# Attention decode gradient on one core: one head in 128 partitions, or two heads in 64 each

## The chip, the cores and the metric

The kernel runs on one core of a Trainium2 chip. The time is the device time in microseconds (us) of one execution. A profiled execution also gives a span, from the first instruction to the last, and a trace of every engine: TensorE (PE; its weight loads are listed as PEld), VectorE (DVE), ScalarE (ACT), GpSimd (POOL), and SyncE (SP), which here does nothing but issue DMA transfers. The transfers run on 16 DMA engines.

## The reference

Attention with a single query per head, and its gradient: 32 heads, 8192 keys, head dimension 128, all in bf16. Of the forward pass the output is returned, of the backward pass dQ, dK and dV.

```python
B, H, Sq, Skv, Dh = 1, 32, 1, 8192, 128

def _fwd_reference(q, k, v):
    scale = q.shape[-1] ** -0.5
    scores = jnp.einsum('bhqd,bhkd->bhqk', q, k) * scale
    attn = _softmax(scores, axis=-1)
    return jnp.einsum('bhqk,bhkd->bhqd', attn, v)
```

For one head, with p the softmax of scale times K q, and g the gradient that comes in: out = p V; dV = p g (an outer product of 8192 by 128); dp = V g; ds = scale times p times (dp minus the sum of p dp); dQ = ds K; dK = ds q (again an outer product). So K and V are read once (2 MB per head each), and dK and dV, just as large, are written: 268.4 MB in all.

## The kernel before, in words

One head at a time. A tile of K or V has 128 partitions of 64 rows (NT) of 128 numbers: partition p holds the rows 64p to 64p + 63 of the head, which lie together in memory, so a transfer is 128 rows of 16 KB. K has three such buffers, V two, and the results G_dk and G_dv have two each.

The program is written in the order in which the engines take it (a manual schedule): each engine works through its own instructions in the order of the text and waits at each for what it needs. A round of the loop over h (line 304) works on head h and finishes the head before it (p_ = h - 1):

- Scores of head h. DVE transposes K in four chunks of 16 rows (`k_blocks`, line 162, into one tile XK with a slice for each chunk), and TensorE multiplies each chunk with q, four matmuls per chunk (`k_scores`, line 177). A window of zeros around the q columns (`q_win`) steers each chunk to its own rows of one accumulator. Between the chunks, DVE takes dp of the head before back from PSUM (`v_back`, line 214), and TensorE sums p dp (`pd_sum`).
- ds of the head before (`ds_of`), its contraction with K for dQ (`dq_of`, line 231), and its outer product with q, in four quarters on DVE (`outer`, line 256), woven between the steps of the softmax of head h: maximum (lines 339 to 350), exponential on ACT (line 355), sum by a matmul with ones (line 356), reciprocal (line 369), p repeated four times along the row for DVE (line 371), and the window for the contraction (line 372).
- V of head h: TensorE transposes it as 32-bit words, 32 blocks of 128 by 128 (`v_transposes`, line 197), ACT copies them from PSUM to the tile XV (`v_copy`, line 188), TensorE contracts p with V (`contract`, line 231) and XV with g (`v_scores`, line 207). Meanwhile DVE makes dV in four quarters (`outer`, line 256) into G_dv.

The accumulators of the output and of dQ stay in PSUM for eight heads (ST), in other rows for each; after every eighth head they are copied and gathered by eight matmuls (`gather_copy`, `gather`, lines 238 to 247).

All large transfers are issued by SP, in the order of the text, and SP waits at each until its tile is free or ready. At the start: K of head 0 in four parts, V 0, K 1, V 1, and soon K 2. Then in each round: store dK of the head before (`outer`, line 266, after the last quarter; halves for the first and the last head), load K of h + 2 (line 81), store dV of h, load V of h + 2 (line 85, before the last quarter of dV). All go through one queue to the 16 DMA engines. A load has to wait until the buffer's last reader is done, a product until the store of the buffer's last content has landed.

Of the kernel before, what the change touches and what calls it, by code (L numbers as in the profile page):

```python
# [14 lines left out]

CH = 16
TB = 4
ST = 8
R = 4
# [6 lines left out]
def kernel(  # L26
# [14 lines left out]
    assert D == P and S % (P * CH) == 0 and H <= P  # L41
    NT = S // P
    NCH = NT // CH
    NQ = P // QD
    assert NCH == 4 and NQ == 4
    W = D // 2
    NB = W // QD
    scale = float(D) ** -0.5
# [4 lines left out]
    ktpool = ctx.enter_context(tc.tile_pool(name="ktp", bufs=1))  # L53
    gpool = ctx.enter_context(tc.tile_pool(name="gen", bufs=2))
    small = ctx.enter_context(tc.tile_pool(name="small", bufs=2))
    xvpool = ctx.enter_context(tc.tile_pool(name="xvp", bufs=1))
    single = ctx.enter_context(tc.tile_pool(name="single", bufs=1))
# [7 lines left out]
    NG = NT // 4  # L65
    NX = NT // 2
    Kt, Vt, XK, XV, st, acc, qd = {}, {}, {}, {}, {}, {}, {}

    def rows_of(x, h, c, parts):
        L = NT // parts  # L70
        return x[0, h].rearrange("(p n) d -> p n d", p=P)[:, c * L:(c + 1) * L, :]
# [5 lines left out]
    def load_k(h):  # L77
        Kt[h] = kpool.tile([P, NT, D], BF16, tag="K", name="Kt")
        parts = NCH if h == 0 else 1
        for c in range(parts):  # L80
            nc.sync.dma_start(slots(Kt[h], c, parts), rows_of(k, h, c, parts))

    def load_v(h):
        Vt[h] = vpool.tile([P, NT, D], BF16, tag="V", name="Vt")
        nc.sync.dma_start(Vt[h][:], rows_of(v, h, 0, 1))
# [7 lines left out]
    load_v(1)  # L93

# [7 lines left out]
    nc.vector.memset(ones_f[:], 1.0)  # L102
    do_win = consts.tile([P, H, 2, QD + 2], BF16)
    nc.gpsimd.memset(do_win[:], 0.0)
    wins = {}
    for which in ("p", "ds"):
        wins[which] = []
        for i in range(2):
            w = consts.tile([P, NG, 2 * QD - 4], BF16, name=f"win_{which}{i}")
            nc.gpsimd.memset(w[:], 0.0)  # L110
            wins[which].append(w)
    q_win = []
    for i in range(2):
        w = consts.tile([P, 2 * NB, P + QD], BF16, name=f"win_q{i}")
        nc.gpsimd.memset(w[:], 0.0)
        q_win.append(w)
# [3 lines left out]

    q_blk = consts.tile([P, H, 2 * NB, NQ], BF16)
    four = consts.tile([H, 2 * NB, NQ, QD], BF16)
# [12 lines left out]
    for c in range(2 * NB):  # L135
        nc.vector.tensor_tensor(
            q_blk[:, :, c, :], tp[:, c, 0:H].unsqueeze(2).to_broadcast([P, H, NQ]),
            in_quad[:].unsqueeze(1).to_broadcast([P, H, NQ]), op=ALU.mult)


    twice = consts.tile([H, 2, 2, W], BF16)

    def do_columns():
        for e2 in range(2):
            nc.scalar.copy(
                twice[:, e2], rows[:, 1, :].rearrange("h (j e) -> h e j", e=2)[:, e2:e2 + 1, :].to_broadcast([H, 2, W]))
        tp = psT.tile([P, 2 * TB, P], BF16, tag="T", name="tp_do")
        for e2 in range(2):
            nc.tensor.transpose(tp[:, e2, 0:H], twice[:, e2].rearrange("h t j -> h (t j)"), ident[0:H, 0:H])
        for e2 in range(2):  # L150
            for t in range(2):
                nc.scalar.copy(do_win[t * W:(t + 1) * W, :, e2, 2 + t], tp[t * W:(t + 1) * W, e2, 0:H])
# [4 lines left out]
    def k_blocks(h, u):  # L157


        if u == 0:  # L160
            XK[h] = ktpool.tile([P, CH, NB, NCH, QD], F32, tag="XK", name="XK_sb")
        nc.vector.transpose(XK[h][:, :, :, u, :],  # L162
                            slots(Kt[h], u, NCH).rearrange("p g d -> p (g d)").bitcast(F32).rearrange(
                                "p (g w j) -> p g w j", g=CH, w=NB))

    def q_window(h):
        nc.scalar.copy(q_win[h % 2][:, :, 2 * NCH - 2:2 * NCH - 2 + P].rearrange("p c (a r) -> p c a r", r=QD)[:, :, :, 0],
                       q_blk[:, h])

    def k_scores(h, u):  # L170
        if u == 0:
            st[h]["s"] = psS.tile([P, 512], F32, tag="s", name="s_ps")
        cols = XK[h].rearrange("p g w u i -> p (g w u i)").bitcast(BF16).rearrange(
            "p (g w u i e) -> p w u e g i", g=CH, w=NB, u=NCH, e=2)
        at = 2 * (NCH - 1 - u)
        for c in range(2 * NB):
            nc.tensor.matmul(st[h]["s"][:], lhsT=q_win[h % 2][:, c, at:at + P], rhs=cols[:, c // 2, u, c % 2],  # L177
                             start=(u == 0 and c == 0), stop=(u == NCH - 1 and c == 2 * NB - 1),
                             skip_group_check=True)

    def s_back(h):
        x = st[h]
        sT = single.tile([P, CH, QD], F32, tag="sT", name="sT")
        nc.vector.transpose(sT[:].rearrange("p g r -> p (g r)"), x["s"][:])  # L184
        x["sn"] = sT[:, :, 0:2 * NCH:2].rearrange("p g u -> p u g")

    def v_copy(h, c):
        nc.scalar.copy(XV[h][:, c * TB:(c + 1) * TB, :], st[h].pop(("T", c))[:])  # L188

    def v_transposes(h, c):  # L190
        if c == 0:
            XV[h] = xvpool.tile([P, NX, P], F32, tag="XV", name="XV_sb")
        T_ps = psT.tile([P, TB, P], F32, tag="T", name="T_ps")
        words = Vt[h].rearrange("p n d -> p (n d)").bitcast(F32)
# [3 lines left out]
        st[h]["T", c] = T_ps  # L198

    def v_scores(h):  # L200
        cols = XV.pop(h).rearrange("p m s -> p (m s)").bitcast(BF16).rearrange(
            "p (m z s e) -> p z e m s", z=2, s=P, e=2)
        out = st[h]["dp"] = psD.tile([P, 512], F32, tag="dp", name="dp_ps")
        for z in range(2):
            for e2 in range(2):
                for b in range(NQ):
                    nc.tensor.matmul(out[b * QD:(b + 1) * QD, :], lhsT=do_win[:, h, e2, 2 - 2 * z:2 - 2 * z + QD],  # L207
                                     rhs=cols[:, z, e2, :, b * QD:(b + 1) * QD],
                                     start=(z == 0 and e2 == 0), stop=(z == 1 and e2 == 1), skip_group_check=True)

    def v_back(h):
        x = st[h]
        x["dpT"] = single.tile([P, NX // 2, QD], F32, tag="dpT", name="dpT")
        nc.vector.transpose(x["dpT"][:].rearrange("p m r -> p (m r)"), x["dp"][:])  # L214
        prod = small.tile([P, NT // 4, 4], F32, tag="prod", name="prod")
        x["pd"] = small.tile([P, 1], F32, tag="pd", name="pd")
        nc.vector.scalar_tensor_tensor(  # L217
            out=prod[:], in0=x["dpT"][:, :, 0:4], scalar=1.0, in1=x["e"][:].rearrange("p (m r) -> p m r", r=4),
            op0=ALU.mult, op1=ALU.mult, accum_out=x["pd"][:])

    def window(h, which):
        return wins[which][h % 2]

    def contract(h, which, first=0, last=NG):
        X, pool = (Vt[h], psO) if which == "p" else (Kt[h], psQ)
        if h % ST == 0 and first == 0:
            acc[which] = pool.tile([P, 512], F32, tag="acc", name="acc_" + which)
        at = QD - 4 - 4 * (h % ST)
        for g in range(first, last):
            b = g % NQ  # L230
            nc.tensor.matmul(acc[which][b * QD:(b + 1) * QD, :], lhsT=window(h, which)[:, g, at:at + QD],  # L231
                             rhs=X[:, 4 * g:4 * g + 4, :].rearrange("p n d -> p (n d)"),
                             start=(h % ST == 0 and g < NQ), stop=(h % ST == ST - 1 and g >= NG - NQ),
                             skip_group_check=True)

    def gather_copy(which):
        S = acc["S" + which] = single.tile([P, 4, D], F32, tag="S", name="S_" + which)
        nc.scalar.copy(S[:].rearrange("p j d -> p (j d)"), acc.pop(which)[:])

    def gather(h, which, bank):  # L240
# [3 lines left out]
        for j in range(4):  # L244
            nc.tensor.matmul(bank[:, at:at + ST], lhsT=S[:, j, :], rhs=pick[:, j, :],
                             start=(j == 0), stop=(j == 3), skip_group_check=True)
        nc.scalar.copy(to[:, h - ST + 1:h + 1], bank[:, at:at + ST])

    def outer(h, which, r):
        x = st[h]  # L250
        if r == 0:
            x[which] = gpool.tile([P, NT, D], BF16, tag=which, name="G_" + which)
        G, dst = x[which], out_2 if which == "dk" else out_3
        rep, row = x["ds"] if which == "dk" else x["p"], qd[h][:, 0 if which == "dk" else 1, :]
        Q = NT // 4
        nc.vector.tensor_tensor(  # L256
            slots(G, r, 4).rearrange("p n (a b) -> p n a b", b=R),
            slots(rep, r, 4).unsqueeze(2).to_broadcast([P, Q, D // R, R]),
            row.rearrange("p (a b) -> p a b", b=R).unsqueeze(1).to_broadcast([P, Q, D // R, R]),
            op=ALU.mult)  # L260
        parts = 1
        if h == 0 or h == H - 1:
            parts = 2
        if r % (4 // parts) == 4 // parts - 1:
            c = r // (4 // parts)
            nc.sync.dma_start(rows_of(dst, h, c, parts), slots(G, c, parts))

    def rows_bc(h, bank):
# [35 lines left out]
    for h in range(H + 1):  # L304
# [16 lines left out]
        if h == 0:  # L321
            do_columns()
# [106 lines left out]
```

## Time and profile before

| | before |
|---|---|
| median of three executions | 642.79 us (642.36 to 643.2) |
| profiled execution | 642.33 us, of which span 640.5 |
| DVE busy | 546.7 us, 85% |
| TensorE busy | 466.5 us, 73%; mean granted clock 0.857 |
| ACT busy | 205.5 us, 32% |
| DMA queue of K, V, dK, dV | 268.46 MB, 98.6% of 16 engines' span |
| rate over the span | 420 GB/s |
| packets | 19,671 |
| K and V loads, 2 MB each | 32 and 31, some 30 us from issue to landing |

An engine that is busy 85% of the time may still be what everything waits for in one stage and not in another, so shares over the whole span say little by themselves. Where a resource is busy 98.6% of the span, as the DMA queue here, the time is its work plus the few us in which it had nothing to do.

### The profile page before, as it was taken

To read this page: it belongs to the slowest core of one execution; us is meant where nothing else is said; L and a number is where in the kernel's file an instruction comes from. 1 tells how busy PE (TensorE), PEld (TensorE's weight loads), DVE (VectorE), ACT (ScalarE), POOL (GpSimd) and SP (SyncE) were. 2 spreads that over 40 slices of the span, in tenths; PEclk is the share of its full clock that TensorE was granted. 3 is DMA by queue.
4 is the path that set the end of the run, shared out by engine and by line. 5 is a ranking of instruction groups with operands and counts; after the bars stand their busy time and mean duration, and the time that the engine had idled before them with its cause. 6 is when DMAs were issued, how large, how long until landed. Compare 5 with 4: busy or idle time off the path is not lost.

```text
span 640.5 us, 8426 instructions
## 1 busy us (share of the span) xinstructions
PE 466.5 (73%) x3336; PEld 276.5 (43%) x3336; DVE 546.7 (85%) x780; ACT 205.5 (32%) x507; POOL 7.1 (1%) x13
## 2 busy tenths in 40 slices
PE   3776778778877867887866867767877687676771
PEld 1444444445544533455533444434554344444351
DVE  6799999998999999988889888898888988889871
ACT  1433332234433322334421333313442133322240
POOL 4000000000000000000000000000000000000000
PEclk9979888887787899877899887898787888879875
DMA  8999999999999999999999999999999999999994
GB/s 353 421 415 427 429 431 426 425 433 426 429 431 427 429 431 427 430 429 429 431 427 432 428 425 437 427 424 436 428 425 435 428 426 434 426 430 433 427 405 193
DMA packets 19671, 269.01 MB, mean 420 GB/s; under 512 B 2352, under 2 KB 2352, under 8 KB 2864
## 3 DMA queue, kind: packets, MB, share of 16 engines
q1 hardware_dynamic: 19536, 268.46, 98.6%
q8 instruction: 26, 0.43, 0.3%
q14 instruction: 13, 0.11, 0.0%
q10 hardware_dynamic: 96, 0.02, 0.0%
HBM read 134.23 MB, written 134.23 MB: 419 GB/s over the span
## 4 chain that ended last, share of the span: by engine, by line
DMA 45%; DVE 39%; PE 9%; ACT 4%; issue 1%; DVEq 0%; ACTq 0%
DMA Kt<-in_k_dram 45%; DVE XK_sb L162 15%; DVE G_dv L256 9%; DVE G_dk L256 7%; PE s_ps L177 3%; DVE dpT L214 2%; PE T_ps L197 2%; PE acc_ds L231 2%; ACT XV_sb L188 2%; DVE sT L184 1%; ACT p_rep L371 1%; DVE prod L217 1%; DVE ds L285 1%; ACT qd L273 1%; DVE four L125 1%
## 5 line engine op out<-in xcount | busy, mean ns | idle before, releaser
L197 PE MATMUL T_ps<-ident_f,Vt 128*128 128x128 f32 x1024 | 178.0, 339 | 1.0 <-DMA Vt<-in_v_dram 0.4
L256 DVE TENSOR_TENSOR G_dv<-p_rep,qd 128x2048 bf16<-128x2048 bf16 x128 | 148.2, 1220 | 35.3 <-DMA out_dram<-G_dv 28.1
L177 PE MATMUL s_ps<-XK_sb,win_q 128*128 128x512 bf16 x512 | 135.8, 397 | 50.1 <-DVE XK_sb L162 26.3
L197 PEld LDWEIGHTS T_ps<-ident_f,Vt 128*128 128x128 f32 x1024 | 151.4, 177 | 28.5 <-issue 20.1
L256 DVE TENSOR_TENSOR G_dk<-ds_rep,qd 128x2048 bf16<-128x2048 bf16 x128 | 154.7, 1210 | 1.1
L188 ACT COPY XV_sb<-T_ps 128x512 f32<-128x512 f32 x256 | 138.4, 586 | 53.2 <-PE T_ps L197 52.6
L162 DVE STREAM_TRANSPOSE XK_sb<-Kt 128x1024 f32<-128x1024 f32 x128 | 151.4, 1221 | 3.1 <-DMA Kt<-in_k_dram 2.9
L177 PEld LDWEIGHTS <-win_q 128*128 128x128 bf16 x512 | 52.7, 105 | 123.8 <-issue 83.2
L290 ACT COPY win_ds<-ds 128x64 bf16<-128x64 bf16 x32 | 7.8, 244 | 193.0 <-DVE ds L285 193.0
L355 ACT ACTIVATE e<-sT,nbias 128x64 f32<-128x64 f32 x32 | 13.0, 406 | 138.4 <-DVE nbias L350 138.4
L343 PE MATMUL m_ps<-ident_f,top 128*128 128x128 f32 x32 | 11.0, 342 | 60.3 <-DVE top L341 57.3
L207 PE MATMUL dp_ps<-XV_sb,do_win 128*32 128x512 bf16 x512 | 34.0, 382 | 24.7 <-ACT XV_sb L188 24.7
L231 PE MATMUL acc_p<-Vt,win_p 128*32 128x512 bf16 x512 | 48.3, 516 | 0.5 <-ACT win_p L372 0.5
L343 PEld LDWEIGHTS m_ps<-ident_f,top 128*128 128x128 f32 x32 | 4.5, 139 | 74.4 <-DVE top L341 72.9
L231 PE MATMUL acc_ds<-Kt,win_ds 128*32 128x512 bf16 x512 | 33.5, 382 | 0.9 <-ACT win_ds L290 0.9
L207 PEld LDWEIGHTS <-do_win 128*32 128x32 bf16 x512 | 14.2, 94 | 36.0 <-issue 29.5
L369 DVE RECIPROCAL rinv<-m_ps 128x1 f32<-128x1 f32 x32 | 5.4, 168 | 24.9 <-ACT qd L273 24.9
L184 DVE STREAM_TRANSPOSE sT<-s_ps 128x512 f32<-128x512 f32 x32 | 22.7, 709 | 3.6 <-PE s_ps L177 3.6
L356 PE MATMUL m_ps<-rs,ones_f 128*128 128x1 f32 x64 | 15.4, 310 | 11.5 <-ACT e L355 11.5
L231 PEld LDWEIGHTS <-win_p 128*32 128x32 bf16 x512 | 13.1, 117 | 23.8 <-issue 12.2
L214 DVE STREAM_TRANSPOSE dpT<-dp_ps 128x512 f32<-128x512 f32 x32 | 21.6, 675 | 0.8 <-PE dp_ps L207 0.8
L356 PEld LDWEIGHTS m_ps<-rs,ones_f 128*128 128x128 f32 x64 | 14.0, 272 | 17.8 <-ACT e L355 17.3
(57 smaller groups left out, 203.3 us busy)
## 6 DMA issues: line engine op xcount, KB each, us to landing
Vt<-in_v_dram SPq DMA_DIRECT2D x32, 2048.0 KB, 29.5
Kt<-in_k_dram SPq DMA_DIRECT2D x31, 2048.0 KB, 31.6
out_dram<-G_dv SPq DMA_DIRECT2D x30, 2048.0 KB, 34.8
out_dram<-G_dk SPq DMA_DIRECT2D x30, 2048.0 KB, 32.2
out_dram<-G_dv SPq DMA_DIRECT2D x4, 1024.0 KB, 11.6
out_dram<-G_dk SPq DMA_DIRECT2D x4, 1024.0 KB, 11.7
Kt<-in_k_dram SPq DMA_DIRECT2D x4, 512.0 KB, 5.6
out_dram<-fin_sb SPq DMA_DIRECT2D x2, 8.0 KB, 12.1
```

The costliest lines, as they stand in the source:

```text
L162: nc.vector.transpose(XK[h][:, :, :, u, :], slots(Kt[h], u, NCH).rearrange("p g d -> p (g d)").bitcast(F32).rearrange("p (g w j) -> p g w ...
L177: nc.tensor.matmul(st[h]["s"][:], lhsT=q_win[h % 2][:, c, at:at + P], rhs=cols[:, c // 2, u, c % 2], start=(u == 0 and c == 0), stop=(u == ...
L184: nc.vector.transpose(sT[:].rearrange("p g r -> p (g r)"), x["s"][:])
L188: nc.scalar.copy(XV[h][:, c * TB:(c + 1) * TB, :], st[h].pop(("T", c))[:])
L197: nc.tensor.transpose(T_ps[:, i, :], words[:, m * P:(m + 1) * P], ident_f[:])
L207: nc.tensor.matmul(out[b * QD:(b + 1) * QD, :], lhsT=do_win[:, h, e2, 2 - 2 * z:2 - 2 * z + QD], rhs=cols[:, z, e2, :, b * QD:(b + 1) * QD ...
L214: nc.vector.transpose(x["dpT"][:].rearrange("p m r -> p (m r)"), x["dp"][:])
L231: nc.tensor.matmul(acc[which][b * QD:(b + 1) * QD, :], lhsT=window(h, which)[:, g, at:at + QD], rhs=X[:, 4 * g:4 * g + 4, :].rearrange("p ...
L256: nc.vector.tensor_tensor(slots(G, r, 4).rearrange("p n (a b) -> p n a b", b=R), slots(rep, r, 4).unsqueeze(2).to_broadcast([P, Q, D // R, ...
L343: nc.tensor.transpose(x["m"][:, 128:256], top[:].to_broadcast([P, P]), ident_f[:])
L355: nc.scalar.activation(e[:].rearrange("p (u g) -> p u g", u=NCH), x["sn"], ACT.Exp, bias=nbias[:], scale=scale, accum_out=rs[:])
L356: nc.tensor.matmul(x["m"][:, 0:1], lhsT=ones_f[:], rhs=rs[:], start=True, stop=True, skip_group_check=True)
```

## The change

Two heads are worked on at once: the view of K, V, dK and dV joins heads 2j and 2j + 1, so that partitions 0 to 63 hold the first and 64 to 127 the second, each with 128 rows (NT = 128), and a transfer has 128 rows of 32 KB, 4 MB in all. There are 16 rounds (HP) and a last one instead of 32 and a last one. A pair has eight chunks (NU) of 16 rows instead of four per head, so the number of chunks, transposes, score matmuls, contractions and outer products over the whole run stays, each of the same size; the softmax steps work on twice the width and are half as many.

K has three buffers and V two, of 4 MB. The result tiles are gone: dV is written over V and dK over K, chunk by chunk, and stored from there. XK has three small tiles, one chunk each, in place of one large one. The work on V is one loop of eight steps: two groups of transposes with their copies, four contractions, then the outer product over that chunk, and after the fourth and eighth step the product with g. Sums over a head use a matrix with ones in two 64 by 64 blocks; windows, bias and broadcast rows are written in two halves. The accumulators are gathered for every pair.

A pair's dK and dV are each stored at once after the eighth chunk (the last pair: dK in four parts, dV in two). SP's order in round j: store dK of pair j - 1, load V of j + 1, store dV of j, load K of j + 2. At the start: K 0, V 0, K 1, V 1, K 2, each whole.

```diff
+XK_BUFS = 3
+PARTS = {("dk", -1): 4, ("dv", -1): 2}
...
-    ktpool = ctx.enter_context(tc.tile_pool(name="ktp", bufs=1))
-    gpool = ctx.enter_context(tc.tile_pool(name="gen", bufs=2))
-    small = ctx.enter_context(tc.tile_pool(name="small", bufs=2))
+    ktpool = ctx.enter_context(tc.tile_pool(name="ktp", bufs=XK_BUFS))
+    small = ctx.enter_context(tc.tile_pool(name="small", bufs=1))
...
-        return x[0, h].rearrange("(p n) d -> p n d", p=P)[:, c * L:(c + 1) * L, :]
+        return x[0, 2 * j:2 * j + 2].rearrange("b s d -> (b s) d").rearrange("(p n) d -> p n d", p=P)[:, c * L:(c + 1) * L, :]
...
     load_v(0)
     load_k(1)
     load_v(1)
+    load_k(2)
...
+    def k_blocks(j, u):
+        XK[j, u] = ktpool.tile([P, CH, NB, QD], F32, tag="XK", name="XK_sb")
+        nc.vector.transpose(XK[j, u][:].rearrange("p g w i -> p (g w i)"),
+                            slots(Kt[j], u, NU).rearrange("p g d -> p (g d)").bitcast(F32))
...
+    def window(which, src):
+        for t in range(2):
+            nc.scalar.copy(wins[which][t * M:(t + 1) * M, :, 4 * t:4 * t + 4], src[t * M:(t + 1) * M])
...
+    def outer(j, which, r):
+        x = st[j]
+        G, dst = (Kt[j], out_2) if which == "dk" else (Vt[j], out_3)
...
+        parts = PARTS.get((which, j - HP), 1)
+        if r % (NU // parts) == NU // parts - 1:
+            c = r // (NU // parts)
+            nc.sync.dma_start(rows_of(dst, j, c, parts), slots(G, c, parts))
...
+            k_blocks(j, 0)
+            k_scores(j, 0)
+        if j > 0:
+            v_back(p_)
+            pd_sum(p_)
+            gather(p_, "p", st[p_]["m"])
+        if j < HP:
+            for u in (1, 2):
+                k_blocks(j, u)
+                k_scores(j, u)
+        if j > 0:
             ds_of(p_)
+        for u in range(3, NU):
+            if j < HP:
+                k_blocks(j, u)
+                k_scores(j, u)
+            if j > 0 and u >= 4:
+                contract(p_, "ds", (u - 4) * DQ, (u - 3) * DQ)
+        if j > 0:
+            gather_copy("ds")
             outer(p_, "dk", 0)
+        if j < HP:
+            s_back(j)
+        if j > 0:
             outer(p_, "dk", 1)
...
+        if j > 0:
+            for r in range(4, NU):
+                outer(p_, "dk", r)
+            if j + 1 < HP:
+                load_v(j + 1)
+        if j == HP:
             break
+        for r in range(NU):
+            v_transposes(j, 2 * r)
+            v_transposes(j, 2 * r + 1)
+            contract(j, "p", 4 * r, 4 * r + 4)
+            if r % 4 == 3:
+                v_scores(j, r // 4)
+            outer(j, "dv", r)
+        gather_copy("p")
+        if j + 1 < HP:
+            do_window(j + 1)
+        if 0 < j and j + 2 < HP:
+            load_k(j + 2)
...
+    result(o_all, out_0)
     result(dq_all, out_1)
```

## The prediction

> **What bounds the kernel now.** First the page: how busy each resource is, and the rate in 40 slices.
>
> ```profile
> PE 466.5 (73%) x3336; PEld 276.5 (43%) x3336; DVE 546.7 (85%) x780; ACT 205.5 (32%) x507; POOL 7.1 (1%) x13
> ...
> GB/s 353 421 415 427 429 431 426 425 433 426 429 431 427 429 431 427 430 429 429 431 427 432 428 425 437 427 424 436 428 425 435 428 426 434 426 430 433 427 405 193
> ...
> q1 hardware_dynamic: 19536, 268.46, 98.6%
> ```
>
> The one queue that carries K, V, dK and dV keeps the 16 DMA engines 98.6% busy. DVE comes second. So I asked for busy time, granted clock, DMA share and rate by stage (the last three columns).
>
> ```profile
> 8.00:24.00 16.00, 12.04 (x69) 6.15 (x69) 9.68 (x19) 7.67 (x21) 0.00 (x0) 1.00 1.01 433
> 26.00:32.00 6.00, 3.90 (x26) 1.52 (x19) 5.97 (x9) 0.00 (x0) 0.00 (x0) 1.00 0.98 408
> ...
> 128.00:192.00 64.00, 52.23 (x384) 32.74 (x385) 58.22 (x81) 25.55 (x63) 0.00 (x0) 0.84 1.01 429
> ...
> 626.00:632.00 6.00, 0.69 (x3) 0.40 (x3) 1.45 (x2) 0.64 (x3) 0.00 (x0) 0.50 0.94 390
> 632.00:634.00 2.00, 0.00 (x0) 0.00 (x0) 0.00 (x0) 0.00 (x0) 0.00 (x0) 0.50 0.24 99
> ...
> 638.00:639.00 1.00, 0.00 (x0) 0.00 (x0) 0.00 (x0) 0.00 (x0) 0.00 (x0) 0.50 0.04 17
> ```
>
> The steady rate is 429 GB/s with no DMA idle time. At the end most engines stop near 632, and a share of 0.04 (under one engine of 16) runs on to 639: the slowest engine trails the mean by some 6 us, and it ends the run. Then the chain of waits, to see whether DVE or DMA sets the pace.
>
> ```profile
> 10.91 6.38 PE s_ps L177 x16
> ...
> 21.91 4.63 DVE G_dv L256 x4
> 26.54 3.41 DVE XK_sb L162 x3
> ...
> 251.94 30.10 DMA Kt<-in_k_dram
> 282.06 3.50 DVE XK_sb L162 x3
> ```
>
> Up to 252 us the chain is nearly all DVE, some 18 us per head (G_dv starts at 21.91, 40.02, 57.99): compute eats the lead of the first loads. From then on each step is a K load of some 30 us: 13 MB, or six transfers, stand queued. The DMA stays full only because loads and stores always wait in its queue. The last view is SP's own instructions, the order of issue at the start.
>
> ```profile
> 5.08 0.33 SPq L81 DMA_DIRECT2D Kt<-in_k_dram  x1
> 24.30 2.61 SPq L266 DMA_DIRECT2D out_dram<-G_dv  x2
> 27.02 1.09 SPq L85 DMA_DIRECT2D Vt<-in_v_dram  x1
> 35.68 0.33 SPq L266 DMA_DIRECT2D out_dram<-G_dk  x1
> ```
>
> The first store of dV is issued at 24.30 and that of dK at 35.68, when the loads issued by 5.08 have only just drained (10.5 MB at 433 GB/s). That handover is where the change bites.
>
> **1. Bytes and rows.** The bytes stay (268.4 MB). Transfers on q1 fall from 137 to 70 (16 K, 16 V, 17 dV, 19 dK, 2 small), rows grow from 16 to 32 KB. What a row costs: with 8 KB rows (last stores, 626 to 632) 390/0.94 = 415 GB/s of busy time, with 16 KB rows 429/1.01 = 425. Per engine that is 316 ns for 8 KB and 617 ns for 16 KB: 14 to 15 ns fixed per row, completion included. A 32 KB row saves one such cost in 1,234 ns, 1.15% of the 631.5 us that the queue was busy: 7.2 us. The shares are rounded; with all rounding one way or the other it is 4 to 11 us. If a 32 KB row is cut into two packets it is near 0. I take 7.2, ends 0 and 11.
> The Trainium skill, "DMA: Bandwidth & Descriptors", section "Where 436 GB/s comes from", puts a ceiling of 435 GB/s on the core's fabric. By that rule, from 429, an estimate of at most 1.4% or 8.7 us is to be had, and the sum below would be 642.1 at best. The same page's "Latency and other measured facts" speaks against growing the pitch between partitions (207 GB/s per direction at 512 KiB, 214 unhampered). Our pitch is 32 KB; read as 3% it would cost an estimated 19 us (a sum of 670 with no saving), and no row of this trace shows such a loss.
>
> **2. The start: one hole.** K(0) now comes as one 4 MB load instead of four of 512 KB. Full rate begins near 2.3 us; 4.19 MB at 433 GB/s land at 12.6 (with 0.5 for completion), where the first DVE transpose ran at 9.15. The small first rows brought 2.11 MB by 8 us; at 433 it would be 2.47, so larger rows give back 0.8 us.
> Iteration 0: the first 16 score matmuls took 6.38 us with TensorE just started; 13.8 + 6.4 + 16 more at 1.03 per four (4.1) = 24.3. From the last score to the finished p window took 4.84 (17.32 to 22.16). Doubled widths, a second reduction, a second broadcast matmul and split window copies add 1.1: 30.3. Then dV over V: DVE's product r must wait until TensorE has read slot r: 8 transposes 1.03 and 4 contractions 0.27, or 1.3 us per r against DVE's 1.16 (4.63/4); the first group of v_scores, now inside the loop, adds 0.78 of waiting for ACT and 1.05. So dV(0) is done at 30.3 + 0.3 + 7 x 1.3 + 1.85 + 1.16 = 42.7. It is stored whole. The five loads keep the DMA busy to 50.8, dV(0) to 60.4 (25.17 MB at 433 from 2.3).
> Iteration 1 up to the end of dK(0), on DVE: one K transpose 1.2; dpT and two products 1.25; two K transposes 2.3; ds 1.25 (its copy twice as long); five K transposes 5.8; dK 0 1.2; wait for the scores, paced by TensorE's 1.03 + 0.53 of contraction per chunk, 1.3; sT 0.7; dK 1, mx, top, dK 2, nbias, dK 3 4.6; the wait of rinv and p_s 1.3; four dK 4.64: 25.5, at 68.2. Only then can SP issue dK(0), a single 4 MB store, and behind it on the same queue stands the load of V(2), although its buffer came free at 60.4: SP waits in order. Some 1.5 us pass from an issue to full rate (0.74 to 2.3 at the start), so the DMA idles from 60.4 to 69.7: 9.3. TensorE at half clock (0.50 to 0.86 in single 2 us windows) would lengthen it; I take 9.9, a little of the half clock, with ends 6 (DVE's waits of 2.6 left out, the shortest latency) and 13 (3 us of half clock). In the old kernel halves were stored and a head was half as long; the DMA share there never fell below 0.90.
>
> **3. The steady part: does compute keep up?** A pair needs 16.78 MB: 38.7 us at 434 GB/s. DVE needs 25.5 to the end of dK and 8 x 1.16 = 9.3 for dV (TensorE reaches dV's last slot earlier, having begun during dK 4 to 7): 34.8. Against 36 us for two heads before, one sT and one dpT (0.7 each) and a dozen small operations go. In-place writing costs nothing as long as that cover of TensorE holds; without it phase B takes TensorE's 12.5 us or more and the period grows by up to 3. So DMA remains the bound by 1 to 4 us per pair and its backlog grows. I followed SP's order (dK, V load, dV, K load): the K load waits for dK of the same iteration, the V load for the previous dV, each with 20 us of queued work ahead of it. After the second iteration no hole follows (dK(1) is ready near 103, queued work reaches 108). XK's three small buffers let DVE run three chunks ahead of TensorE, and it is that far ahead at most: nothing. The accumulators are now gathered every pair, 32 gathers instead of 8, 1.06 each on TensorE (eight matmuls, L245): that of dQ runs beside a dK product, that of the output between pd_sum and the second chunk of scores, beside two K transposes (2.3 against 0.5 + 1.06 + 0.2 of copy); without that cover up to 1 us per pair, inside the margin. ACT at 32% takes the split window copies: nothing. SP has half the issues, and its small output stores moved to the end stand behind data anyway: nothing.
>
> **4. The end.** When V(15) lands some 39 us of stores and loads are still to move; dV(15) in two and dK(15) in four parts are ready before their turn. In the old kernel the share was 0.87 from 620 to 632, 1.6 us lost by the mean engine, but the last engine ran on. I take 0.6, ends 0 and 2.
>
> **The sum**, against the profiled execution's 642.33 us (span 640.5, 1.83 around it; the median of three is 642.79): + 9.9 - 7.2 - 0.8 - 0.6 = + 1.3: 643.6.
>
> **The rivals.**
> *The rows pay more than the hole costs* (faster). Saving 11, hole 6 to 7, tail 2: 642.33 - 7 = 635. For it: the 8 KB windows at 415 and 416 (408/0.98) agree on a price per row. Against: the rate varies by 1% between windows anyway, and the hole is in the program's order.
> *Compute becomes the bound* (slower). If the period passes 38.7 us, the time is 42.7 + 15 periods + 18 for the last dK and its store. At 40 us: 661 span, 662 in all; 39 gives 648. It would come from TensorE: the clock was 0.82 to 0.89 over stages of 64 us, and phase B at half clock is 1.9 + 0.5 per r, 19 us instead of 10. For it: DVE's product now waits for TensorE eight times per pair. Against: 4 us of margin, and TensorE was slow for only some 4 us per head.
> *Reads and in-place writes are ordered too coarsely* (slower): transposes of r + 1 wait for dV's write of r. Period 34.8 + 7 = 42, 690 in all. Against: XK's interleaved slices were written three at a time (3.41 us) while TensorE read others.
> *The rows are cut or bring nothing*: 642.33 + 9.9 - 1.4 = 651.
>
> **How the numbers follow.** My forecast, hole and saving nearly cancelling (637 to 650): 0.60, of which 0.18 below, 0.17 inside, 0.25 above the 0.2% (1.3 us) that a measurement can tell from no change. The rows pay more: 0.16, faster. Compute bound: 0.14. Coarse ordering: 0.03. Nothing from rows: 0.07. Faster 0.34, same 0.17, slower 0.49. The range reaches from 635 (little of the first rival left out) to 655, which leaves out coarse ordering and most of the compute-bound cases.
>
> **What would show it.** Right: some 10,000 packets instead of 19,671; 432 to 435 GB/s in steady stages; one stage near 60 to 70 us with a DMA share near zero; K transposes or V transposes waiting for their loads from the middle of the run. Wrong: 18,000 packets, or 429 GB/s as before (no saving); a DMA share under 0.98 after 110 us, and DVE waiting on TensorE in dV (compute bound); no stage without traffic (no hole).

## The result, and the profile after

The changed kernel takes 647.48 us (four runs, 647.44 to 648.2), the old one 642.66 us beside it. The ratio is 1.0077, with a 95% interval of 1.0059 to 1.0094: slower by 4.8 us. The forecast was 643.6 with a range of 635 to 655, and slower as the likeliest sign. The profiled execution took 647.51 us, of which the span is 645.7.

The page of the changed kernel, the lines that answer to those shown of the old one:

```profile
PE 506.6 (78%) x3480; PEld 284.4 (44%) x3480; DVE 513.9 (80%) x658; ACT 219.9 (34%) x504; POOL 3.2 (0%) x10
...
GB/s 385 428 422 328 287 394 431 439 422 432 431 427 431 435 427 417 439 427 429 440 425 427 445 424 427 442 427 425 439 429 427 442 427 431 437 425 430 341 435 283
DMA packets 10022, 269.01 MB, mean 417 GB/s; under 512 B 1280, under 2 KB 1280, under 8 KB 1280
...
q1 hardware_dynamic: 9888, 268.46, 97.3%
```

The packets halved, so a row of 32 KB is one packet. The queue was busy 97.3% of 645.7 us, or 628.3, against 631.5 before: 3.2 us less work. Yet it was idle 17.4 us against 9.0. DVE has 33 us less to do, and it does not matter. Two dips stand out in the rates: slices four and five, and the third from the end. By stage (granted clock, DMA share and GB/s are the last three columns):

```profile
60.00:64.00 4.00, 2.56 (x16) 2.23 (x17) 2.87 (x6) 1.24 (x5) 0.00 (x0) 0.71 0.37 158
64.00:68.00 4.00, 3.82 (x19) 2.67 (x17) 3.96 (x6) 3.06 (x7) 0.00 (x0) 0.50 0.00 0
68.00:72.00 4.00, 3.60 (x37) 2.20 (x40) 4.00 (x4) 2.73 (x5) 0.00 (x0) 0.94 0.62 262
320.00:384.00 64.00, 54.77 (x386) 30.75 (x385) 53.40 (x65) 24.43 (x54) 0.00 (x0) 0.83 1.00 432
600.00:612.00 12.00, 8.78 (x53) 6.66 (x50) 11.48 (x16) 5.94 (x13) 0.00 (x0) 0.72 0.71 304
638.00:640.00 2.00, 0.00 (x0) 0.00 (x0) 0.00 (x0) 0.00 (x0) 0.00 (x0) 0.50 1.00 418
640.00:642.00 2.00, 0.00 (x0) 0.00 (x0) 0.00 (x0) 0.00 (x0) 0.00 (x0) 0.50 0.38 151
```

A share is counted by the packets that start in a stage, so it can pass 1. Between 60 and 72 us the mean engine loses 4 x (0.63 + 1.00 + 0.38) = 8.0 us, and 3.5 us between 600 and 612. At the end nearly all engines stop together near 641, with a few last rows until 642.5; in the old kernel one trailed to 639 when most had stopped at 632. The issues by SP show what the hole at 60 us is:

```profile
44.19 0.35 SPq L261 DMA_DIRECT2D out_dram<-Vt  x1
68.99 0.34 SPq L261 DMA_DIRECT2D out_dram<-Kt  x1
69.43 0.38 SPq L84 DMA_DIRECT2D Vt<-in_v_dram  x1
```

dV(0) went out at 44.19 and dK(0) at 68.99, forecast for 42.7 and 68.2, and V(2) behind it. From 140 us on the chain of waits is DMA again:

```profile
532.54 21.34 DMA out_dram<-Kt
553.94 29.36 DMA Kt<-in_k_dram
583.32 1.26 DVE XK_sb L161
```

A store of dK lands, only then is the buffer's next K loaded, and DVE waits for that K. The last line is the start of the last pair: its K lands at 583.3, and everything after it is that pair's compute and the drain.

### The profile page after: what moved, and what is told of

It reads as the page before. It is cut to its first block, busy times and chain, and to the rows that moved or that the text cites. A ratio compares the mean times of both kernels' runs of the same rounds, so it can differ in the third digit from the quotient of the medians.

```text
span 645.7 us, 8436 instructions
## 1 busy us (share of the span) xinstructions
PE 506.6 (78%) x3480; PEld 284.4 (44%) x3480; DVE 513.9 (80%) x658; ACT 219.9 (34%) x504; POOL 3.2 (0%) x10
## 3 DMA queue, kind: packets, MB, share of 16 engines
q1 hardware_dynamic: 9888, 268.46, 97.3%
## 4 chain that ended last, share of the span: by engine, by line
DMA 51%; PE 28%; DVE 14%; ACT 5%; issue 1%; DVEq 0%; SPq 0%; ACTq 0%
DMA Kt<-in_k_dram 29%; DMA out_dram<-Kt 21%; PE s_ps L171 13%; DVE Kt L253 6%; PE T_ps L188 5%; DVE XK_sb L161 4%; PE m_ps L245 3%; PE acc_ds L232 2%; PE acc_p L232 2%; DVE sT L178 1%; DMA out_dram<-fin_sb 1%; ACT p_rep L364 1%; ACT e L352 1%; ACT win_p L224 1%; PE dp_ps L202 1%
## 5 line engine op out<-in xcount | busy, mean ns | idle before, releaser
L171 PE MATMUL s_ps<-XK_sb,q_win 128*128 128x512 bf16 x512 | 161.5, 461 | 45.0 <-DVE XK_sb L161 44.1
L253 DVE TENSOR_TENSOR Vt<-p_rep,qd 128x2048 bf16<-128x2048 bf16 x128 | 152.6, 1223 | 24.8 <-PE acc_p L232 18.6
L188 PEld LDWEIGHTS T_ps<-ident_f,Vt 128*128 128x128 f32 x1024 | 135.8, 164 | 38.1 <-issue 23.4
L253 DVE TENSOR_TENSOR Kt<-ds_rep,qd 128x2048 bf16<-128x2048 bf16 x128 | 150.6, 1211 | 1.4 <-PE acc_ds L232 0.9
L171 PEld LDWEIGHTS <-q_win 128*128 128x128 bf16 x512 | 54.5, 116 | 140.9 <-issue 117.5
L238 ACT COPY S_ds<-acc_ds 128x512 f32<-128x512 f32 x16 | 9.4, 585 | 141.7 <-PE acc_ds L232 141.7
L178 DVE STREAM_TRANSPOSE sT<-s_ps 128x512 f32<-128x512 f32 x16 | 11.5, 717 | 27.4 <-PE s_ps L171 27.4
L245 PE MATMUL m_ps<-lane,S_p 128*128 128x2 f32 x128 | 24.7, 315 | 0.0
L245 PEld LDWEIGHTS m_ps<-lane,S_p 128*128 128x128 f32 x128 | 24.1, 280 | 0.0
L245 PEld LDWEIGHTS m_ps<-lane,S_ds 128*128 128x128 f32 x128 | 18.5, 220 | 1.6 <-ACT S_ds L238 1.6
```

What stands on the lines that cost most here:

```text
L171: nc.tensor.matmul(st[j]["s"][:], lhsT=q_win[:, c, at:at + P], rhs=cols[:, c // 2, c % 2], start=(u == 0 and c == 0), stop=(u == NU - 1 an ...
L188: nc.tensor.transpose(T_ps[:, i, :], words[:, m * P:(m + 1) * P], ident_f[:])
L245: nc.tensor.matmul(bank[:, at:at + 2], lhsT=S[:, i, :], rhs=pick[:, i, 0:2], start=(i == 0), stop=(i == 3), skip_group_check=True)
L253: nc.vector.tensor_tensor(slots(G, r, NU).rearrange("p n (a b) -> p n a b", b=R), slots(rep, r, NU).unsqueeze(2).to_broadcast([P, CH, D // ...
```

## The experiments

Each is an edit of the changed kernel, timed beside the old one. The difference given is that of the median to the changed kernel's 647.48 us; the ratio is to the old kernel, with its 95% interval. The old kernel's median beside them was 642.38 to 642.58 us (642.66 beside the changed kernel), so differences of 0.3 us mean nothing.

### V(2) ahead of dK(0)

```diff
+        if j == 1:
+            load_v(2)
         if j < HP:
             x = st[j] = {}
...
-            if j + 1 < HP:
+            if 1 < j and j + 1 < HP:
                 load_v(j + 1)
```

> The load of V(2) is issued by SP at the start of the second round, ahead of the store of dK(0) instead of behind it; nothing else changes. In the changed kernel its buffer was free when dV(0) had landed (about 61 us), but SP issued it at 69.43, behind dK(0) at 68.99, and the DMA share was 0.00 from 63 to 69. Theory (the order on SP makes the hole, and the run is bound by the DMA queue afterwards): V(2) is issued near 62, traffic from 63 on, dK(0) queues behind it; 6 to 8 us off the time, 640 to 641.5. Rival (the later rounds are a loop of dK store, K load and compute that absorbs any lead): the hole closes but the time stays within 1.5 us of 647.5.

Measured: 645.02 us, 2.5 less; ratio 1.0032 (1.0019 to 1.0044). Neither figure came. SP's issues:

```profile
44.42 0.35 SPq L261 DMA_DIRECT2D out_dram<-Vt  x1
64.81 0.33 SPq L84 DMA_DIRECT2D Vt<-in_v_dram  x1
69.24 0.34 SPq L261 DMA_DIRECT2D out_dram<-Kt  x1
79.79 0.34 SPq L261 DMA_DIRECT2D out_dram<-Vt  x1
89.47 0.34 SPq L80 DMA_DIRECT2D Kt<-in_k_dram  x1
```

V(2) could not go at 62, because its buffer is free only when the store of dV(0) has landed. The trace records 16 completions for that store, as many as there are engines: 13 of them come from 61.66 to 62.43, two near 63.2 and only the last at 64.73, while the mean engine runs dry at 61. And K(3), which waits for dK(0) to land, went at 89.47 instead of 82.02. So the order on SP is part of the hole, but a load moved ahead pushes the next one back. The last K load was issued at 551.70 instead of 553.94, and the span shrank from 645.7 to 643.5, by as much.

### All transfers in halves of 16 KB rows

```diff
-        nc.sync.dma_start(Kt[j][:], rows_of(k, j))
+        for c in range(2):
+            nc.sync.dma_start(slots(Kt[j], c, 2), rows_of(k, j, c, 2))
```

V loads likewise; stores of 4 MB as two of 2 MB.

> Each 4 MB load and store is issued as two transfers of 2 MB one after the other, with rows of 16 KB (every 32 KB); order, buffers and compute stay. Theory of the prediction (a fixed 14 to 15 ns per row and engine): +7 us, 654 to 655, some 18,000 packets. By the busy time of the queue in the two traces (631.5 against 628.3 us, 0.8 of it from the small first rows): +2 to +3 us, about 650. Rival (the row size does nothing): within 1 us of 647.5.

Measured: 644.23 us, 3.25 less instead of more; ratio 1.0026 (1.0017 to 1.0036). All three expectations fell, because the edit did two things: it made the rows smaller, and it let halves go ahead. A load or a store of a half waits only for its half, so DVE started on half of K(0), half of dV(0) went out at 32.67 and half of dK(0) at 58.52, and there was no hole:

```profile
60.00:64.00 4.00, 3.83 (x21) 2.23 (x20) 4.00 (x4) 3.01 (x7) 0.00 (x0) 0.51 1.01 430
64.00:68.00 4.00, 3.61 (x42) 2.21 (x40) 4.00 (x5) 2.23 (x5) 0.00 (x0) 1.00 1.01 430
```

The price of the rows shows in the queue's busy time, 98.3% of 642.2 = 631.3 us, 3.0 more. A pair of kernels below, neither with the hole, compares the rows again.

### Two buffers for the last output rows

```diff
-        fin_sb = small.tile([H, D], BF16, tag="fin", name="fin_sb")
+        fin_sb = small.tile([H, D], BF16, tag="fin", name="fin_sb", bufs=2)
```

> The small tile of the last two output rows (fin_sb) gets two buffers instead of one; nothing else changes. In the changed kernel ACT waited 9.98 us with the copy of dQ until the store of the output row had landed (643.26), and the second small store was issued after all data had moved. Theory (this wait lies on the end): both small stores are issued near 636 and land with the last of dK, 2 to 3 us off: 644.5 to 645.5. Rival (the small store would have waited for the queue anyway): under 0.7 us.

Measured: 646.23 us, 1.25 less; ratio 1.0053 (1.004 to 1.0065). The timeline of the changed kernel at its end:

```profile
635.74 0.33 SPq L261 DMA_DIRECT2D out_dram<-Kt  x1
636.16 7.70 SPq L297 DMA_DIRECT2D out_dram<-fin_sb  x2
643.26 0.25 ACT L296 COPY fin_sb<-fin_ps 32x128 bf16<-32x128 bf16 x1 [9.98 <-DMA out_dram<-fin_sb]
```

The change set the pool of small tiles to one buffer, so the copy of the dQ row waited 9.98 us for the output row's store to land, and its own store came after all data. The wait lay on the end, as the first expectation had it, but it was worth half of the 2 to 3 us.

### dK of the last pair but one in four parts

```diff
-PARTS = {("dk", -1): 4, ("dv", -1): 2}
+PARTS = {("dk", -1): 4, ("dv", -1): 2, ("dk", -2): 4}
```

> dK of the last pair but one is stored in four parts instead of one; nothing else changes. In the changed kernel the DMA share was 0.71 from 600 to 612 us, before dK(14) was issued at 610.19 as a whole: 3.5 us lost by the mean engine. Theory (the slowest of the 16 engines still had work, since K(15) landed only at 583.3 with 29 us queued behind it, and it ends the run): the share rises above 0.9, the time falls by under 1 us. Rival (the mean engine decides): 3 to 4 us off, 643.5 to 644.5.

Measured: 648.56 us, 1.1 more; ratio 1.0088 (1.0075 to 1.01). No expectation had a loss, and no run shows its cause. The stages of this kernel:

```profile
600.00:612.00 12.00, 8.69 (x67) 6.28 (x60) 11.51 (x16) 6.74 (x15) 0.00 (x0) 0.86 0.97 412
612.00:628.00 16.00, 12.62 (x116) 7.87 (x119) 11.80 (x18) 5.79 (x13) 0.00 (x0) 0.81 0.92 390
628.00:634.00 6.00, 2.42 (x22) 1.31 (x14) 6.00 (x6) 1.34 (x5) 0.00 (x0) 0.78 0.85 354
```

The hole between 600 and 612 closed and came back as shares of 0.92 and 0.85 further on. Bytes sent earlier there buy nothing: the last K landed at 583.45, as before.

### dK of the first pair in eight parts

```diff
-PARTS = {("dk", -1): 4, ("dv", -1): 2}
+PARTS = {("dk", -1): 4, ("dv", -1): 2, ("dk", -16): 8}
```

> Only dK of the first pair is stored in eight parts of 512 KB, each as soon as its product is done (56 to 69 us), instead of at 69 as a whole. Theory (the whole store leaves the DMA engines without work from 61 to 69): the hole shrinks from 8 us to about 2 us of the mean engine; 4 to 6 us off 647.5, 641.5 to 643.5. Rival (as when V(2) was moved ahead, where 4.2 us of the hole closed and 2.4 us came off the time: most of a lead is given back later): 645 to 646.

Measured: 644.56 us, 2.9 less; ratio 1.0032 (1.002 to 1.0043), outside both ranges. The parts went out from 56.70 to 69.8 and the hole nearly closed (DMA share 0.92 and 0.96 from 60 to 68 us), and the profiled execution of this kernel was 4.2 us shorter than that of the changed kernel (span 641.5), its last K load issued 4.25 us earlier. But that execution was the fastest of seven; the median stands for 2.9.

### K of the first pair in four loads: one part undone

```diff
-        nc.sync.dma_start(Kt[j][:], rows_of(k, j))
+        parts = 4 if j == 0 else 1
+        for c in range(parts):
+            nc.sync.dma_start(slots(Kt[j], c, parts), rows_of(k, j, c, parts))
```

> Undoes one part of the change: K of the first pair comes in four loads of 1 MB, so that DVE starts on the first quarter instead of at 13.2 us. Theory: the scores start near 10.5 instead of 14.5, all of the first two rounds moves 3 to 4 us ahead, dK(0) is issued near 65 and the hole shrinks by as much: 643.5 to 644.5. Rival (the setup of the q window and TensorE's slow start hold the first round back anyway): within 1 us of 647.5.

Measured: 641.68 us, 5.8 less; ratio 0.9989 (0.998 to 0.9998). Undoing this part alone makes up more than the whole loss of 4.8 us. SP's issues:

```profile
38.79 0.35 SPq L263 DMA_DIRECT2D out_dram<-Vt  x1
64.21 0.34 SPq L263 DMA_DIRECT2D out_dram<-Kt  x1
64.64 0.38 SPq L86 DMA_DIRECT2D Vt<-in_v_dram  x1
```

dV(0) goes out 5.4 us earlier and dK(0) 4.8 us earlier; the small rows of q, now ahead of less K, land earlier too, and the first K transpose runs at 5.88 instead of 13.16. The lead reached the end undiminished: the last K load was issued at 549.25, 4.7 us earlier. The 5.8 us are well above the expected 3 to 4; the profiled execution, the slowest of eleven, has 4.5 less than that of the changed kernel. The hole did not close: the DMA share was 0.38 from 60 to 64 and 0.92 from 64 to 72 us, or 3.1 us lost instead of 8.0.

### Stores in halves, loads whole

```diff
-        parts = PARTS.get((which, j - HP), 1)
+        parts = PARTS.get((which, j - HP), 2)
```

> Every dK and dV is stored in two halves (rows of 16 KB), the first after the fourth product; loads stay at 4 MB and 32 KB rows. Theory: the hole closes, since half of dK(0) is issued near 63, and so does that near 604 to 612, while half of the bytes pay the price of 16 KB rows that the queue's busy time showed with all transfers halved (631.3 against 628.3 us, so 1.5): 642 to 644. Rival (halved loads, which land and free buffers earlier, were what made the kernel with all transfers halved faster): 646 to 648.

Measured: 644.88 us, 2.6 less; ratio 1.0032 (1.0019 to 1.0045), between the two expectations. Half of dK(0) went out at 64.03, three us after the queue had run dry, so the hole was only cut in two. With loads halved too half of dK(0) had gone out at 58.52, before the queue ran dry; those 5.5 us are those of the earlier start on K(0) (half of dV(0) 32.67 against 38.17), not of freed buffers, since no buffer had yet been used twice. The queue's busy time is 98.0% of 643.9 = 631.0 us, nearly that with all transfers halved, though only the stores have smaller rows; why was not tried.

### Without the hole

K of the first pair in four loads, dK of the first pair in eight stores, two buffers for the last rows (the edits above together).

> K of the first pair in four loads, dK of the first pair stored in eight parts, two buffers for the last output rows; all else with 32 KB rows. Theory: no hole at the start, 1.2 us off the end, the busy time of 32 KB rows kept: 638.5 to 641, faster than both kernels. Rival (a lead is mostly given back at the end, where the last pair's work takes 52 us from the landing of its K): 642 to 644.

Measured: 637.97 us, 9.5 less; ratio 0.9925 (0.9913 to 0.9938): faster than both kernels. By stage:

```profile
60.00:64.00 4.00, 3.83 (x24) 2.43 (x23) 4.00 (x5) 2.85 (x6) 0.00 (x0) 0.62 0.90 375
64.00:68.00 4.00, 3.61 (x40) 2.08 (x39) 4.00 (x5) 2.15 (x4) 0.00 (x0) 1.00 1.03 422
...
628.00:632.00 4.00, 0.00 (x0) 0.00 (x0) 0.00 (x0) 0.00 (x0) 0.00 (x0) 0.50 1.03 428
632.00:636.00 4.00, 0.00 (x0) 0.00 (x0) 0.00 (x0) 0.00 (x0) 0.00 (x0) 0.50 0.11 39
```

If 1.25 us of the 9.5 belong to the end, as measured above, the hole was worth 8.3 us, very near the 8.0 of DMA time that it showed.

### The same with 16 KB rows

All other loads and stores of the kernel without the hole in two halves.

> The kernel without the hole (K of the first pair in four loads, dK of the first pair in eight stores, two small output buffers; 638.0 us), with every other 4 MB transfer cut into two of 2 MB with rows of 16 KB. No hole at 60 us in either, so the difference is the rows' and the halves'. Theory (the price that the queue's busy time showed, 631.3 against 628.3 us): 3 us more, 640 to 642. By the prediction's 14 to 15 ns per row: 7 us more, 644 to 646. Rival (halves start stores and free buffers earlier, which is worth as much as the rows): 637 to 639.

Measured: 643.27 us, 5.3 more than with 32 KB rows; ratio to the old kernel 1.0015 (1.0006 to 1.0024). None of the three figures: between the first two. The queue's busy time is 98.4% of 641.6 = 631.3 us against 98.8% of 636.3 = 628.7, 2.6 more. The rest is in the last stages:

```profile
628.00:632.00 4.00, 0.00 (x0) 0.00 (x0) 0.00 (x0) 0.00 (x0) 0.00 (x0) 0.50 0.81 337
632.00:636.00 4.00, 0.00 (x0) 0.00 (x0) 0.00 (x0) 0.00 (x0) 0.00 (x0) 0.50 0.15 62
636.00:638.00 2.00, 0.00 (x0) 0.00 (x0) 0.00 (x0) 0.00 (x0) 0.00 (x0) 0.50 0.06 25
638.00:640.00 2.00, 0.00 (x0) 0.00 (x0) 0.00 (x0) 0.00 (x0) 0.00 (x0) 0.50 0.06 25
```

A share of 0.06 is one engine of 16. Such a share lasts to 640 here, as it did in the old kernel to 639; with whole 32 KB rows it is shorter (with only K(0) cut 1.5 us, from 636 to 637.5). So the mean engine pays 2.6 us and the slowest one some 5. Halves are also twice as many transfers and start earlier, so the 5.3 us are the price of rows and transfers together, less what the earlier starts bring.

### Finer stores of the last two pairs

```diff
-PARTS = {("dk", -1): 4, ("dv", -1): 2, ("dk", -16): 8}
+PARTS = {("dk", -1): 8, ("dv", -1): 4, ("dk", -16): 8, ("dk", -2): 4}
```

> The same kernel without the hole (638.0 us); only the stores of the last two pairs are finer: dK of the last pair but one in four parts, of the last pair in eight instead of four, dV of the last pair in four instead of two. In all runs so far the span ended 90.3 to 92.2 us after the last K load was issued. Theory (after that landing the last pair's compute, some 53 us to its last dK product, sets the end, and only the drain behind it can shrink): 1 to 1.5 us off, 636.5 to 637. Rival (the slowest DMA engine's queue sets the end): no change, 637.5 to 638.5. Second rival (bytes moved earlier at the end shorten the run): 3 us off, 635.

Measured: 638.05 us, the same as without it (637.97); ratio 0.9934 (0.992 to 0.9947). The theory that compute sets the end and only its drain can shrink is not borne out. No change is what the slowest engine's queue would give: the mean engine ran out of work earlier (share 0.84 from 628 to 632 us against 1.03), yet the last engine moved rows to 635.7 against 634.5. But the trace does not say which engine moved a row, and the finer stores also have smaller rows (12,758 packets against 11,462), whose price may have cancelled a gain; so that is argued and not shown.

## Why the prediction was right, and where it was not

The time fell into a wide range, and the sign that came was given 0.49. As measured below, the terms that the forecast had make + 2.2 us of the + 4.8; the other 2.6 it did not have.

**The hole** was right in place and mechanism, down to the issue times. It was sized at 9.9 us, from 60.4 to 69.7; the mean engine lost 8.0, and the time 8.3. The half clock that I added for did come (0.50 from 64 to 68 us), and dK(0) was only 0.8 us later than worked out. The 0.8 us at the start came too (rate over the first 24 us 394 GB/s against 378), but not clearly from the 32 KB rows: with K(0) in four loads of 8 KB rows it was 394 as well. What step 2 did not see is that K(0) as one load was a larger cause of the hole than the order on SP: it named a delay of 3.5 us, and four loads brought the first transpose forward by 7.3 us and took 5.8 us off the time.

**The rows** were right in direction, and mis-sized. A fixed cost per row of 14 to 15 ns was to save 7.2 us of busy time; the busy time fell by 3.2, and the time by 5.3 where the hole is out of the way. The busy time itself is good to about 1 us: the kernel with V(2) ahead, with the same rows as the changed one, has 97.8% of 643.5 = 629.3. The traces' records of single rows give the cost: in the median 309 ns for 8 KB, 611 for 16 and 1213 for 32, so 7 to 9 ns that do not grow with the row. In the mean less is left, 614 ns in the old kernel against 1225 in the changed one, mostly because one row of 32 KB in a hundred takes over 1.6 us. The forecast's price came from the last stage, where 8 KB rows drain while engines run out of work; that is a poor place to read a rate. The rate rose to 432 GB/s only in the second half of the run (431 from 100 to 576 us, 429 in the old kernel), not to 434. Under the ceiling of the Trainium skill ("DMA: Bandwidth & Descriptors", "Where 436 GB/s comes from") an estimate of up to 8.7 us was to be had; the runs show 2.6 to 3.2 of it in busy time. The loss at large pitches that the same page has under "Latency and other measured facts" did not appear at 32 KB: no stage of 64 us between 128 and 576 us was below 429 GB/s.

**The end** failed. It was to gain 0.6 us. The slowest engine's lag shrank from some 7 us (632 to 639) to under 2 (641 to 642.5), which I had not forecast, but I overlooked that one buffer for all small tiles puts the last dQ row behind the output row's store, 1.25 us; and the last pair begins only when its K has landed, so that the span ended 90.3 to 92.2 us after the last K load's issue in every kernel with whole loads, whatever was done to stores there. In the old kernel it was 73.1 us (567.39 to 640.5).

**The steady part** was right: DMA share 1.00 from 100 to 600 us, DVE waiting for K and never the reverse, no coarse ordering of in-place writes. DVE did wait 18.6 us in all for TensorE's reads of V; the queue's backlog hid it.

**The sum**: + 8.3 for the hole, - 5.3 for the rows, - 0.8 at the start and + 1.25 for the small buffer make + 3.45, against + 4.8 measured; 1.35 is left over. The kernel without the hole and with 16 KB rows shows it too: 0.9 us above the old kernel's 642.38 beside it, though its start is better. It would fit the longer tail behind the last K, where shares of 0.71 to 0.92 appear, but no run separated it. Against the forecast's + 1.3: rows 1.9 too large, 0.6 at the end that did not come, 1.25 left out, the 1.35 left over, less 1.6 too much for the hole.

## What to carry to other kernels

Where DMA is the bound, look for the moment when the queue runs dry, not at the rate: at the start, follow the first load to the first product to the first store, in SP's order, and cut the first load and the first late store even if whole transfers are better everywhere else. A load that waits for a store waits for the slowest engine, here until 64.8 us when the mean one was idle from 61. When a pool's buffers are cut to one, check its last, smallest users too.

## What the runs showed of the hardware that I had not expected

With 16 KB rows one DMA engine ran on alone at the end in each of the three kernels that used them throughout: read in steps of half a us, the share was 0.04 to 0.08 from 635.5 to 639 us in the old kernel, from 634.5 to 638.5 with all halves, and from 634.5 to 640 without the hole in halves, 3.5 to 5.5 us. With 32 KB rows such a stretch was 1.5 us at most (2.5 with the finer last stores). The queue's mean busy time differs by some 0.4% only. Which engine it is and why it falls behind was not tried.

A lead won in the first 70 us reached the end nearly whole when it made the last K load earlier (4.7 us of issue time and 4.5 of span with K(0) cut), though some 30 us of transfers stood queued all the time in between.
